# Window attention feeding a Mish FFN: attention matmuls in runs over two pairs of heads, two runs a chunk

## The chip, the cores and the metric

The kernel runs on one core of a Trainium2 chip. The metric is the device time of one execution in microseconds (us). The engines are called by their short names: PE (TensorE matmul; PEld is its weight load), DVE (VectorE), ACT (ScalarE), POOL (GpSimd) and SP (SyncE, which issues the DMAs).

## The reference

Sliding-window attention over q, k, v of 8 batches, 8 heads, 576 positions and 64 channels, and then a feed-forward network over the 4608 tokens of 512 channels:

```
mask = (rel >= 0) & (rel < 64)                 # a window of 64 positions
attn = softmax(where(mask, q @ k.T / 8, -1e9))  # sum + 1e-9 in the denominator
x    = (attn @ v) as [4608 tokens, 512 channels]
h    = x @ w_in                                 # 512 -> 2048
out  = (h * tanh(log1p(exp(h)))) @ w_out        # Mish, 2048 -> 512
```

All is in fp32. The kernel splits each FFN operand in a high and a low part (`xh`/`xl`, `wi_h`/`wi_l`, `gh`/`gl`, `wo_h`/`wo_l`) and sums three products of them.

## The kernel before, in words

The tokens are cut into 12 chunks of 384. A chunk has 16 FFN steps (f = 0 to 15). One step is 12 matmuls of `ffn_in` (L252) into one of two PSUM banks named `h_ps`, two Mish evaluations on ACT (L265, L266), a subtraction on POOL (L267), and, two steps later (`LAG`), 9 matmuls of `ffn_out` (L270) into the three accumulators `acc0`, `acc1`, `acc2`. So in step n of a chunk the matmuls that close the chunk before (its f = 15) run in step 1, and those with f = 0 of the new chunk open the accumulators again in step 2. In between `ffn_store` (L278) copies the accumulators to tiles `o`: ACT takes `acc0` and `acc2` (L283), DVE takes `acc1` (L285), and SP writes them out (L286).

The attention of chunk c is worked out while the FFN of chunk c-1 runs. From chunk 4 on it goes in "runs" (L178 to L213): the heads come in pairs, a chunk has 4 pairs with 3 squares of 128x128 scores each, and a run takes 4 squares of each of the two heads of a pair. `run_scores` puts 16 matmuls into two full banks of the pool `ps_at` (3 banks in all). `probs` (L143) takes each square: DVE adds the mask and finds the maximum (L161), ACT takes the exponential (L164), and then DVE normalises all at once (L151 to L153). `run_transpose` (L190) does a 32x32-block transpose on DVE (L193) into a tile `tr`, and `moves` (L186, L187) has SP issue 12 small DMAs from `tr` into `pT`. `run_values` (L196) then does 16 matmuls with `pT` into one bank `o_ps`, which ACT casts to `xh` (L212) and DVE subtracts to `xl` (L213).

The places of all these in the FFN's steps are fixed by `plan_runs` (L369): three runs a chunk, and the values of one run stand right ahead of the scores of the next, after `ffn_in` of a step and ahead of its `ffn_out`. The first run for a chunk stands three steps ahead of the chunk boundary (`ahead = 6` half steps), so the step order after it is: step 13, run, 14, 15, then 0, 1, 2 of the next chunk.

The tiles `pr` (L184), `tr` (L192), `o` (L280) and the staging of weights (L290) share one ring of three buffers in SBUF, tag `st`: a new tile takes the buffer that was handed out three tiles earlier, and its first writer waits for that tile's last reader. The readers of a `tr` are its 12 DMAs. In a run's order the ring hands out `pr`, `tr`; at a chunk boundary `o`, `o`, `o` for `acc0`, `acc1`, `acc2`. So the `o` for `acc2` gets the buffer of the `tr` of the run three steps ahead of the boundary.

Of the kernel before, what the change touches and what calls it, by code (L numbers as in the profile page):

```python
# [10 lines left out]
F32 = mybir.dt.float32  # L11
# [16 lines left out]
def tile_window_attn_mish_ffn(  # L28
# [44 lines left out]
    firsts = []  # L73
# [12 lines left out]
    SQ = DO // P
    pT_all = const.tile([P, 2 * HM * P], F32, name="pT")
    nc.gpsimd.memset(pT_all, 0.0)

    def pT_of(i, squares):  # L90
        n = squares * P
        return pT_all[:, i * n:(i + 1) * n].rearrange("p (r j i) -> p r j i", r=P // 32, i=32)

    pTs = itertools.cycle(pT_of(i, HM) for i in range(2))


    order = []
# [2 lines left out]
    def pe(*args, **kw):  # L100
        order.append(nc.tensor.matmul(*args, **kw).ins)  # L101
# [41 lines left out]
    def probs(c, s_ps, ms, pr, halves=False):  # L143

        ns = len(ms)
        mx = ap_.tile([P, 2 * SQ], F32, name="mx", bufs=3)
        sm = ap_.tile([P, 2 * SQ], F32, name="sm", bufs=3)

        def normal(js):
# [3 lines left out]
            nc.vector.tensor_tensor(pr[:, js, :], pr[:, js, :], sm[:, js].unsqueeze(2).to_broadcast([P, w, P]), ALU.mult)  # L153

        for h in range(2):
            for i, m in enumerate(ms):
                first = [(c * NB + 2 * m + par) % blocks_per_seq == 0 for par in range(2)]
                mk = firsts[first.index(True)] if any(first) else mask
                j = h * ns + i

                nc.vector.tensor_tensor_reduce(  # L161
                    out=pr[:, j, :], in0=s_ps[h][:, i, :], in1=mk,
                    op0=ALU.add, op1=ALU.min, scale=-0.125, scalar=3.0e38, accum_out=mx[:, j:j + 1])
                nc.scalar.activation(pr[:, j, :], pr[:, j, :], AF.Exp, bias=mx[:, j:j + 1], scale=-1.0,  # L164
                                     accum_out=sm[:, j:j + 1])
            if halves:
                normal(slice(h * ns, (h + 1) * ns))
        if not halves:
            normal(slice(0, 2 * ns))
        return pr  # L170

    def att_scores(c, p, tiles):
        s_ps = [bank(c, p, "s_ps").rearrange("p (m k) -> p m k", k=P) for _ in range(2)]
        for m in range(NM):
            products(tiles, m, [s[:, m, :] for s in s_ps])
        return probs(c, s_ps, range(NM), ap_.tile([P, HM, P], F32, name="pr", bufs=2), c == 0)

    def run_scores(c, i, qk):  # L178

        s_ps = [ps_at.tile([P, DO], F32, name="s_ps", tag="at").rearrange("p (m k) -> p m k", k=P) for _ in range(2)]  # L180
        ms = range(i * SQ, (i + 1) * SQ)
        for j, m in enumerate(ms):
            products(qk[m // NM], m % NM, [s[:, j, :] for s in s_ps])
        return probs(c, s_ps, [m % NM for m in ms], mp.tile([P, 2 * SQ, P], F32, name="pr", tag="st", bufs=3))  # L184

    def moves(pT, tr):  # L186
        return [nc.sync.dma_start(pT[k:k + 32, r // 32, :, :], tr[r:r + 32, k // 32, :, :])  # L187
                for r in range(0, P, 32) for k in range(0, P, 32) if 0 <= k - r % BLK <= BLK]

    def run_transpose(pr):  # L190
        pT = pT_of(0, 2 * SQ)
        tr = mp.tile([P, P // 32, 2 * SQ, 32], F32, name="tr", tag="st", bufs=3)  # L192
        nc.vector.transpose(tr.rearrange("p k j i -> p j k i"), pr.rearrange("p j (k i) -> p j k i", i=32))  # L193
        return pT, moves(pT, tr)

    def run_values(i, vs, pT, x):  # L196
        pT, moved = pT
        o_ps = ps_at.tile([P, DO], F32, name="o_ps", tag="at")
        for j in range(SQ):
            m = i * SQ + j  # L200
            for par in range(2):
                n = 2 * (m % NM) + par
                for h in range(2):
                    rows = slice(h * BLK, (h + 1) * BLK)
                    pe(o_ps[rows, (2 * j + par) * BLK:(2 * j + par + 1) * BLK], vs[m // NM][:, n, rows],
                       pT[:, 2 * par:2 * par + 2, h * SQ + j, :], start=True, stop=True)
                    for d in moved:
                        tc.add_manual_dep(order[-1], d.ins.name, SYNC, reason="values in one piece")
                    moved = []
        xh, xl = (t.rearrange("p c n -> p (c n)")[:, i * DO:(i + 1) * DO] for t in x)  # L210
        with tc.high_priority(offset=SOON):
            nc.scalar.copy(xh, o_ps)  # L212
            nc.vector.tensor_tensor(xl, o_ps, xh.bitcast(F32), ALU.subtract)  # L213

    def att_transpose(c, p, pr):
        pT = next(pTs)
# [15 lines left out]
        return pT, []  # L232

    def att_values(c, p, v_t, pT, x):
        pT, moved = pT
        xh, xl = x
        o_ps = bank(c, p, "o_ps")
        for n in range(NB):
            m, par = n // 2, n % 2
            for h in range(2):  # L240
                rows = slice(h * BLK, (h + 1) * BLK)
                pe(o_ps[rows, n * BLK:(n + 1) * BLK], v_t[:, n, rows],
                   pT[:, 2 * par:2 * par + 2, h * NM + m, :], start=True, stop=True)

                for d in moved:
                    tc.add_manual_dep(order[-1], d.ins.name, SYNC, reason="values in one piece")
                moved = []
# [66 lines left out]
    class Att:  # L314
# [30 lines left out]
                att_values(self.c, p, self.v[p], self.pT.pop(p), self.x)  # L345
            self.load(p + 2, "v")

        def run_scores(self, i):
            with in_order():
                self.pr[i] = run_scores(self.c, i, self.qk)  # L350
            self.load(i + 2, "qk")
            if i == RUNS - 1:
                self.load(NPAIR + 1, "qk")

        def run_transpose(self, i):
            if self.c == 4 and i == 0:
                nc.gpsimd.memset(pT_of(0, 2 * SQ), 0.0)
            self.pT[i] = run_transpose(self.pr.pop(i))

        def run_values(self, i):  # L360
            if self.x is None:
                self.x = tuple(xp.tile([P, NC_, CH], F32R, name=f"x{n}{self.c % 2}") for n in "hl")
            with in_order():
                run_values(i, self.v, self.pT.pop(i), self.x)
            self.load(i + 2, "v")
            if i == RUNS - 1:
                self.load(NPAIR + 1, "v")
# [141 lines left out]
```

## Time and profile before

| what | value |
|---|---|
| median of 3 timed runs | 952.58 us (951.73 to 952.84) |
| the profiled execution's own time | 954.34 us |
| its span, first to last instruction | 952.6 us |
| mean granted TensorE clock | 0.980 |
| HBM traffic over the span | 69 GB/s |

How to read the profile's lines: a group line gives the source line, engine, operation, output and input tiles and shapes, then count, total busy time, mean of one. A timeline line gives the start in us from the span's start, the duration, and what it is; `x12` means twelve like instructions that follow each other. The chain of waits is the chain of work that ended last, followed back from the end. A matmul in fp32 counts as two passes, so a run's 16 matmuls appear as `x32`.

### The profile page before, as it was taken

What the parts mean: (1) busy time and instruction counts of PE and PEld (TensorE: products, weight loads), DVE (VectorE), ACT (ScalarE), POOL (GpSimd) and SP (SyncE); (2) the same over time, 40 slices, a digit from 0 to 9 for tenths busy, and PEclk for the clock granted to TensorE, in tenths of its full rate; (3) what the DMA queues carried; (4) which work ended last, traced back from release to release, by engine and by line L of the source; (5) the groups of instructions that cost most, each with busy time, mean ns of one, the idle gap of its engine ahead of it and who ended that gap; (6) DMA issues with size and microseconds to landing.
All of it is one profiled execution on the core that took longest, in us unless ns stands there. A gap on an engine that the chain in (4) does not pass through costs nothing.

```text
span 952.6 us, 16654 instructions
## 1 busy us (share of the span) xinstructions
PE 917.1 (96%) x6408; PEld 816.4 (86%) x6408; DVE 301.0 (32%) x960; ACT 430.6 (45%) x1140; POOL 242.0 (25%) x241
## 2 busy tenths in 40 slices
PE   3779999999999999999999999999999999999998
PEld 2668999878889888899988998899988889988996
DVE  6899886142332122122122122222222222220000
ACT  4475333565654444344344345444444444442211
POOL 2234565202121222222222222222222222222221
PEclk9579999999999999999999999999999999999999
DMA  7454341131322222122023123122222222210000
GB/s 249 154 178 165 132 133 45 52 120 64 93 87 85 70 69 85 43 87 94 20 83 101 37 71 101 52 70 85 69 71 68 86 68 70 83 31 7 34 1 34
DMA packets 78031, 77.25 MB, mean 81 GB/s; under 512 B 8832, under 2 KB 69248, under 8 KB 77952
## 3 DMA queue, kind: packets, MB, share of 16 engines
q1 hardware_dynamic: 77952, 76.19, 25.6%
q8 instruction: 51, 0.84, 0.4%
q14 instruction: 28, 0.23, 0.1%
HBM read 56.10 MB, written 9.44 MB: 69 GB/s over the span
## 4 chain that ended last, share of the span: by engine, by line
PE 92%; DVE 4%; ACT 1%; DMA 1%; SPq 1%; issue 0%; ACTq 0%
PE h_ps L101 42%; PE acc L101 42%; PE o_ps L101 4%; PE s_ps L101 3%; DMA st<-w_in 1%; DVE pr L153 1%; DVE wa L301 1%; DVE pr L161 1%; ACT pr L164 1%; DVE wa L302 1%; SPq L187 0%; PE t_ps L228 0%; DVE wi_l L304 0%; ACT L164 0%; ACT L265 0%
## 5 line engine op out<-in xcount | busy, mean ns | idle before, releaser
L267 POOL TENSOR_TENSOR gl<-t,gh 128x384 fp32r<-128x384 f32 x192 | 199.0, 1037 | 614.4 <-ACT gh L266 606.0
L265 ACT ACTIVATE t<-h_ps 128x384 f32<-128x384 f32 x192 | 94.4, 491 | 396.7 <-PE h_ps L101 395.2
L101 PE MATMUL h_ps<-xh,wi_h 128*128 128x384 f32 x768 | 261.2, 340 | 0.0
L101 PE MATMUL h_ps<-xh,wi_l 128*128 128x384 f32 x768 | 260.3, 339 | 0.0
L101 PE MATMUL h_ps<-xl,wi_h 128*128 128x384 f32 x768 | 259.2, 337 | 0.0
L101 PE MATMUL acc<-wo_h,gh 128*128 128x512 f32 x576 | 230.3, 400 | 0.0
L101 PE MATMUL acc<-wo_l,gh 128*128 128x512 f32 x576 | 227.2, 394 | 0.0
L101 PE MATMUL acc<-wo_h,gl 128*128 128x512 f32 x576 | 224.6, 391 | 0.0
L101 PEld LDWEIGHTS h_ps<-xh,wi_h 128*128 128x128 f32 x768 | 145.3, 189 | 9.1 <-issue 0.7
L101 PEld LDWEIGHTS h_ps<-xl,wi_h 128*128 128x128 f32 x768 | 145.3, 189 | 7.2
L101 PEld LDWEIGHTS h_ps<-xh,wi_l 128*128 128x128 f32 x768 | 145.1, 189 | 0.0
L101 PEld LDWEIGHTS acc<-wo_h,gl 128*128 128x128 f32 x576 | 108.4, 188 | 24.6
L101 PEld LDWEIGHTS acc<-wo_h,gh 128*128 128x128 f32 x576 | 108.2, 188 | 22.3 <-issue 5.0
L101 PEld LDWEIGHTS acc<-wo_l,gh 128*128 128x128 f32 x576 | 108.6, 189 | 14.9
L164 ACT ACTIVATE pr<-pr,mx 128x128 f32<-128x128 f32 x288 | 111.7, 389 | 16.0 <-DVE mx L161 15.6
L213 DVE TENSOR_TENSOR xl<-o_ps,xh 128x512 fp32r<-128x512 f32 x24 | 16.6, 692 | 307.2 <-ACT xh L212 307.2
L266 ACT ACTIVATE gh<-h_ps 128x384 fp32r<-128x384 f32 x192 | 93.2, 485 | 0.0
L161 DVE CUSTOM_DVE_ANT_0 pr<-s_ps,mask 128x128 f32<-128x128 f32 x288 | 64.2, 286 | 32.2 <-PE s_ps L101 32.2
L285 DVE COPY o<-acc 128x512 f32<-128x512 f32 x12 | 8.3, 692 | 195.8 <-PE acc L101 195.8
L101 PE MATMUL s_ps<-k_t,q_t 64*64 64x128 f32 x1152 | 48.1, 292 | 13.5 <-DMA k_t<-kT 11.1
L101 PEld LDWEIGHTS o_ps<-pT,v_t 128*64 128x64 f32 x1152 | 40.8, 147 | 17.2 <-issue 8.6
L101 PEld LDWEIGHTS s_ps<-k_t,q_t 64*64 64x64 f32 x1152 | 36.6, 141 | 20.3 <-issue 8.4
(42 smaller groups left out, 572.1 us busy)
## 6 DMA issues: line engine op xcount, KB each, us to landing
v_t<-vN SPq DMA_DIRECT2D x48, 384.0 KB, 3.7
k_t<-kT SPq DMA_DIRECT2D x47, 224.0 KB, 4.1
out<-o SPq DMA_DIRECT2D x36, 256.0 KB, 2.1
pT<-tr SPq DMA_DIRECT2D x288, 32.0 KB, 1.8
q_t<-qT SPq DMA_DIRECT2D x47, 192.0 KB, 3.7
st<-w_in SPq DMA_DIRECT2D x16, 512.0 KB, 4.2
st<-w_out SPq DMA_DIRECT2D x16, 512.0 KB, 3.4
pT<-tr SPq DMA_DIRECT2D x48, 24.0 KB, 1.8
```

Source lines behind the costliest of these rows:

```text
L101: order.append(nc.tensor.matmul(*args, **kw).ins)
L153: nc.vector.tensor_tensor(pr[:, js, :], pr[:, js, :], sm[:, js].unsqueeze(2).to_broadcast([P, w, P]), ALU.mult)
L161: nc.vector.tensor_tensor_reduce(out=pr[:, j, :], in0=s_ps[h][:, i, :], in1=mk, op0=ALU.add, op1=ALU.min, scale=-0.125, scalar=3.0e38, acc ...
L164: nc.scalar.activation(pr[:, j, :], pr[:, j, :], AF.Exp, bias=mx[:, j:j + 1], scale=-1.0, accum_out=sm[:, j:j + 1])
L213: nc.vector.tensor_tensor(xl, o_ps, xh.bitcast(F32), ALU.subtract)
L265: nc.scalar.activation(t, h_ps, AF.Mish)
L266: nc.scalar.activation(gh, h_ps, AF.Mish)
L267: nc.gpsimd.tensor_tensor(gl, t, gh.bitcast(F32), ALU.subtract)
L285: nc.vector.tensor_copy(o, acc[t])
L301: nc.vector.scalar_tensor_tensor(a, hi, 0xC0000000, a, ALU.bitwise_and, ALU.bitwise_or)
L302: nc.vector.scalar_tensor_tensor(a, lo, 29, a, ALU.logical_shift_right, ALU.bitwise_or)
```

## The change

From chunk 4 on a run covers two whole pairs of heads (6 squares a head), and there are two runs a chunk in place of three.

- The scores need three banks. `run_scores` takes two full banks of `ps_at`, and for the remaining two squares of each head one more bank of `ps_at` for one head and one of the two `h_ps` banks for the other. It is 24 matmuls.
- The values are 24 matmuls. The first four blocks of 64 columns go to a bank of `ps_at`, the other eight to an `h_ps` bank. DVE copies and subtracts the first part; ACT casts and DVE subtracts the second, as before.
- `probs` is called for the second pair of the run first, with the squares in the `h_ps` bank leading, and then for the first pair. Each call normalises its own 6 squares.
- The tile `pr` leaves the ring `st` for a pool of its own (2 buffers); `tr` stays in the ring. A run has two transposes, two `tr` tiles and 24 DMAs of 24 KB where it had 12 of 32 KB.
- `pT` is two fixed tiles instead of one tile cut in two ways; its second clearing goes.
- `plan_runs` spaces the two runs evenly. The first still stands three steps ahead of the chunk boundary; the second moves to five steps behind it. Before, the second and third stood two and eight steps behind it.

The core of the diff:

```diff
-    def run_scores(c, i, qk):
-        s_ps = [ps_at.tile([P, DO], F32, name="s_ps", tag="at").rearrange("p (m k) -> p m k", k=P) for _ in range(2)]
-        ms = range(i * SQ, (i + 1) * SQ)
...
-        return probs(c, s_ps, [m % NM for m in ms], mp.tile([P, 2 * SQ, P], F32, name="pr", tag="st", bufs=3))
+    def run_scores(c, qk):
+        full, half = [], []
+        names = ["s_ps"] * 2
+        full = [squares(ps_at.tile([P, DO], F32, name=n, tag="at")) for n in names]
+        half = [squares(pool.tile([P, DO], F32, name=n, tag=tag)) for n, pool, tag in
+                zip(names, (ps_at, ps_h), ("at", "h_ps"))]
...
+        late = [(h, m) for h in (1, 0) for m in (1, 2)] + [(0, 0), (1, 0)]
+        second = probs(c, s_ps[1], [late])
+        return [probs(c, s_ps[0], [sum(HEADS, [])]), second]
...
-        tr = mp.tile([P, P // 32, 2 * SQ, 32], F32, name="tr", tag="st", bufs=3)
+        pT = next(pTs)
+        tr = mp.tile([P, P // 32, HM, 32], F32, name="tr", tag="st", bufs=3)
...
+        o_ps = [ps_at.tile([P, DO], F32, name="o_ps", tag="at")[:, :cut], ps_h.tile([P, DO], F32, name="o_ps", tag="h_ps")]
...
+        value_products(vs[0], pTs_[0], blocks[:NB])
         with tc.high_priority(offset=SOON):
-            nc.scalar.copy(xh, o_ps)
-            nc.vector.tensor_tensor(xl, o_ps, xh.bitcast(F32), ALU.subtract)
+            nc.vector.tensor_copy(xh[:, :cut], o_ps[0])
+            nc.vector.tensor_tensor(xl[:, :cut], o_ps[0], xh[:, :cut].bitcast(F32), ALU.subtract)
+        value_products(vs[1], pTs_[1], blocks[NB:])
+        with tc.high_priority(offset=SOON):
+            nc.scalar.copy(xh[:, cut:], o_ps[1])
+            nc.vector.tensor_tensor(xl[:, cut:], o_ps[1], xh[:, cut:].bitcast(F32), ALU.subtract)
...
+        def run_transpose(self, p):
+            for q in (p, p + 1):
+                self.pT[q] = run_transpose(self.pr.pop(q))
...
-            at = [begin + 2 * round((end - begin) * i / RUNS / 2) for i in range(RUNS + 1)]
-            for i in range(RUNS):
+            step = (end - begin) / (NPAIR // 2)
+            for p in range(0, NPAIR, 2):
+                at = begin + p // 2 * step
+                events.extend([(at, 2, self.run_scores, p), (at + 0.4 * step, 1, self.run_transpose, p),
+                               (at + step, 0, self.run_values, p)])
```

Two places in the order of instructions are shown, since the prediction rests on them. The first is SP's queue around a chunk boundary of the kernel before: a run's 12 moves into `pT` stand ahead of the three writes of `o`.

```order
L187 DMA pT<-tr 32x256 x12
L131 DMA v_t<-vN 128x6x128 x2
L122 DMA q_t<-qT 128x384
L124 DMA k_t<-kT 128x448
L187 DMA pT<-tr 32x256 x12
L286 DMA out<-o 128x512 x3
L131 DMA v_t<-vN 128x6x128
```

The same place in the changed kernel, where the two `pT` tiles have numbers:

```order
L190 DMA pT_106<-tr 32x192 x12
L190 DMA pT_107<-tr 32x192 x12
L126 DMA v_t<-vN 128x6x128 x2
L117 DMA q_t<-qT 128x384
L119 DMA k_t<-kT 128x448
L117 DMA q_t<-qT 128x384
L119 DMA k_t<-kT 128x448
L190 DMA pT_106<-tr 32x192 x12
L190 DMA pT_107<-tr 32x192 x12
L287 DMA out<-o 128x512 x3
```

Between the transposes of the run ahead of a boundary and the writes of `o` there are now 24 moves on SP where there were 12. The second place is ACT's queue at the same boundary, with the counters that each instruction waits for (`DMAHW0` to `7` count landings of SP's DMAs, the others count an engine's instructions; the number behind a tile's name tells allocations apart). Before, with `t` and `gh` the two Mish evaluations of a step:

```order
L265 ACTIVATE t<-h_ps 128x384 [waits PE_49]
L266 ACTIVATE gh<-h_ps 128x384 [waits Pool_49]
L283 COPY o<-acc_3051 128x512 [waits DMAHW4_49,DMAHW3_49,DMAHW5_49,DMAHW2_49,DMAHW6_49,DMAHW1_49,DMAHW7_49,DMAHW0_49,PE_49]
L283 COPY o<-acc_3053 128x512 [waits DMAHW3_49,DMAHW4_49,DMAHW2_49,DMAHW5_49,DMAHW1_49,DMAHW6_49,DMAHW0_49,DMAHW7_49,DVE_49,PE_49]
L265 ACTIVATE t<-h_ps 128x384 [waits PE_49]
L266 ACTIVATE gh<-h_ps 128x384 [waits Pool_49]
```

In the changed kernel:

```order
L266 ACTIVATE t<-h_ps 128x384 [waits PE_49]
L267 ACTIVATE gh<-h_ps 128x384 [waits Pool_49]
L284 COPY o<-acc_3027 128x512 [waits DMAHW4_49,DMAHW3_49,DMAHW5_49,DMAHW2_49,DMAHW6_49,DMAHW1_49,DMAHW7_49,DMAHW0_49,PE_49]
L266 ACTIVATE t<-h_ps 128x384 [waits PE_49]
L267 ACTIVATE gh<-h_ps 128x384 [waits Pool_49]
L284 COPY o<-acc_3029 128x512 [waits DMAHW4_49,DMAHW3_49,DMAHW5_49,DMAHW2_49,DMAHW6_49,DMAHW1_49,DMAHW7_49,DMAHW0_49,DVE_49]
L266 ACTIVATE t<-h_ps 128x384 [waits PE_49]
```

The copy of `acc2` (here `acc_3053` and `acc_3029`) waited for DMAs in both. In both, the ring `st` gives its `o` the buffer of the last `tr` of the run ahead of the boundary, so the landings that it waits for are those of that `tr`: the 12th move before, the 24th now. The two Mish evaluations of step 2 moved ahead of this copy.

More of the change, by code (lines that the diff above doesn't have):

```diff
@@ L83, in tile_window_attn_mish_ffn @@
     wo_l = const.tile([P, NF, DO], F32R, name="wo_l")
[L86 to L94, printed above, removed]
+    pTs = [const.tile([P, P // 32, HM, 32], F32, name=f"pT{i}") for i in range(2)]
+    for t in pTs:
+        nc.gpsimd.memset(t, 0.0)
+    pTs = itertools.cycle(pTs)
     order = []
@@ L141, in products, with probs @@
                q_t[rows, n * BLK:(n + 1) * BLK], k_t[rows, n * BLK:n * BLK + P], start=True, stop=True)
[L143 to L149, printed above, removed]
+    def probs(c, s_ps, turns):
+        pr = ap_.tile([P, HM, P], F32, name="pr", bufs=2)
+        mx = ap_.tile([P, HM], F32, name="mx", bufs=3)
+        sm = ap_.tile([P, HM], F32, name="sm", bufs=3)
+        for turn in turns:
+            js = [h * NM + m for h, m in turn]
+            for j, (h, m) in zip(js, turn):
+                first = [(c * NB + 2 * m + par) % blocks_per_seq == 0 for par in range(2)]
+                mk = firsts[first.index(True)] if any(first) else mask
+                nc.vector.tensor_tensor_reduce(
+                    out=pr[:, j, :], in0=s_ps[h][m], in1=mk,
+                    op0=ALU.add, op1=ALU.min, scale=-0.125, scalar=3.0e38, accum_out=mx[:, j:j + 1])
+                nc.scalar.activation(pr[:, j, :], pr[:, j, :], AF.Exp, bias=mx[:, j:j + 1], scale=-1.0,
+                                     accum_out=sm[:, j:j + 1])
+            js = slice(min(js), max(js) + 1)
             w = js.stop - js.start
@@ L153, in normal @@
             nc.vector.tensor_tensor(pr[:, js, :], pr[:, js, :], sm[:, js].unsqueeze(2).to_broadcast([P, w, P]), ALU.mult)
[L155 to L167, printed above, removed]
@@ L168, in probs, with squares @@
-        if not halves:
-            normal(slice(0, 2 * ns))
-        return pr
+        return pr
+    HEADS = [[(h, m) for m in range(NM)] for h in range(2)]
+    def squares(bank_):
+        return bank_.rearrange("p (m k) -> p m k", k=P)
     def att_scores(c, p, tiles):
-        s_ps = [bank(c, p, "s_ps").rearrange("p (m k) -> p m k", k=P) for _ in range(2)]
+        s_ps = [squares(bank(c, p, "s_ps")) for _ in range(2)]
+        s_ps = [[s[:, m, :] for m in range(NM)] for s in s_ps]
         for m in range(NM):
-            products(tiles, m, [s[:, m, :] for s in s_ps])
@@ L176, in att_scores @@
-        return probs(c, s_ps, range(NM), ap_.tile([P, HM, P], F32, name="pr", bufs=2), c == 0)
-    def run_scores(c, i, qk):
-        s_ps = [ps_at.tile([P, DO], F32, name="s_ps", tag="at").rearrange("p (m k) -> p m k", k=P) for _ in range(2)]
-        ms = range(i * SQ, (i + 1) * SQ)
-        for j, m in enumerate(ms):
-            products(qk[m // NM], m % NM, [s[:, j, :] for s in s_ps])
-        return probs(c, s_ps, [m % NM for m in ms], mp.tile([P, 2 * SQ, P], F32, name="pr", tag="st", bufs=3))
+            products(tiles, m, [s[m] for s in s_ps])
@@ new lines, in att_scores @@
+        return probs(c, s_ps, HEADS if c == 0 else [sum(HEADS, [])])
+    def run_scores(c, qk):
[4 more added lines that the diff above has]
+                zip(names, (ps_at, ps_h), ("at", "h_ps"))]
+        s_ps = [[[full[h][:, m, :] for m in range(NM)] for h in range(2)],
+                [[full[h][:, NM, :]] + [half[h][:, m, :] for m in range(NM - 1)] for h in range(2)]]
+        for tiles, s in zip(qk, s_ps):
+            for m in range(NM):
+                products(tiles, m, [s[h][m] for h in range(2)])
+        late = [(h, m) for h in (1, 0) for m in (1, 2)] + [(0, 0), (1, 0)]
+        second = probs(c, s_ps[1], [late])
+        return [probs(c, s_ps[0], [sum(HEADS, [])]), second]
@@ L190, in run_transpose, with value_products @@
     def run_transpose(pr):
-        pT = pT_of(0, 2 * SQ)
-        tr = mp.tile([P, P // 32, 2 * SQ, 32], F32, name="tr", tag="st", bufs=3)
+        pT = next(pTs)
+        tr = mp.tile([P, P // 32, HM, 32], F32, name="tr", tag="st", bufs=3)
         nc.vector.transpose(tr.rearrange("p k j i -> p j k i"), pr.rearrange("p j (k i) -> p j k i", i=32))
         return pT, moves(pT, tr)
-    def run_values(i, vs, pT, x):
+    def value_products(v_t, pT, blocks):
         pT, moved = pT
[L198 to L210, printed above, removed]
-        with tc.high_priority(offset=SOON):
-            nc.scalar.copy(xh, o_ps)
-            nc.vector.tensor_tensor(xl, o_ps, xh.bitcast(F32), ALU.subtract)
@@ new lines, in value_products, with run_values @@
+        for n, to in enumerate(blocks):
+            m, par = n // 2, n % 2
+            for h in range(2):
+                rows = slice(h * BLK, (h + 1) * BLK)
+                pe(to[rows, :], v_t[:, n, rows], pT[:, 2 * par:2 * par + 2, h * NM + m, :], start=True, stop=True)
+                for d in moved:
+                    tc.add_manual_dep(order[-1], d.ins.name, SYNC, reason="values in one piece")
+                moved = []
+    def run_values(p, vs, pTs_, x):
+        cut = 2 * CH - DO
+        o_ps = [ps_at.tile([P, DO], F32, name="o_ps", tag="at")[:, :cut], ps_h.tile([P, DO], F32, name="o_ps", tag="h_ps")]
+        blocks = [o[:, n:n + BLK] for o in o_ps for n in range(0, o.shape[1], BLK)]
+        xh, xl = (t.rearrange("p c n -> p (c n)")[:, p * CH:(p + 2) * CH] for t in x)
+        value_products(vs[0], pTs_[0], blocks[:NB])
+        with tc.high_priority(offset=SOON):
+            nc.vector.tensor_copy(xh[:, :cut], o_ps[0])
[4 more added lines that the diff above has]
+            nc.vector.tensor_tensor(xl[:, cut:], o_ps[1], xh[:, cut:].bitcast(F32), ALU.subtract)
@@ L234, in att_values @@
     def att_values(c, p, v_t, pT, x):
-        pT, moved = pT
         xh, xl = x
         o_ps = bank(c, p, "o_ps")
[L238 to L247, printed above, removed]
+        value_products(v_t, pT, [o_ps[:, n:n + BLK] for n in range(0, CH, BLK)])
         with tc.high_priority(offset=SOON):
@@ L346, in values, with run_scores, run_values @@
             self.load(p + 2, "v")
-        def run_scores(self, i):
+        def run_scores(self, p):
+            ps = (p, p + 1)
             with in_order():
[L350 to L360, printed above, removed]
+                self.pr.update(zip(ps, run_scores(self.c, [self.qk[q] for q in ps])))
+            for q in ps:
+                self.load(q + 2, "qk")
+        def run_transpose(self, p):
+            for q in (p, p + 1):
+                self.pT[q] = run_transpose(self.pr.pop(q))
+        def run_values(self, p):
             if self.x is None:
                 self.x = tuple(xp.tile([P, NC_, CH], F32R, name=f"x{n}{self.c % 2}") for n in "hl")
+            ps = (p, p + 1)
             with in_order():
[L364 to L367, printed above, removed]
+                run_values(p, [self.v[q] for q in ps], [self.pT.pop(q) for q in ps], self.x)
+            for q in ps:
+                self.load(q + 2, "v")
         def plan_runs(self, begin, end):
-            at = [begin + 2 * round((end - begin) * i / RUNS / 2) for i in range(RUNS + 1)]
-            for i in range(RUNS):
-                events.extend([(at[i], 2, self.run_scores, i), (at[i] + 0.6 * (at[i + 1] - at[i]), 1, self.run_transpose, i),
-                               (at[i + 1], 0, self.run_values, i)])
+            step = (end - begin) / (NPAIR // 2)
[3 more added lines that the diff above has]
+                               (at + step, 0, self.run_values, p)])
         def plan(self, begin, step, turn=0.6, lag=1):
@@ L382, in tile_window_attn_mish_ffn @@
     events = []
-    RUNS = NPAIR * NM // SQ
     def run(slot):
```

## The prediction

> **What bounds the kernel now.** I read the page first: its span, its busy shares, and the chain that ended last.
>
> ```profile
> span 952.6 us, 16654 instructions
> PE 917.1 (96%) x6408; PEld 816.4 (86%) x6408; DVE 301.0 (32%) x960; ACT 430.6 (45%) x1140; POOL 242.0 (25%) x241
> PE 92%; DVE 4%; ACT 1%; DMA 1%; SPq 1%; issue 0%; ACTq 0%
> ```
>
> PE is the chain. The stretch from 100 us to the end, where the change lies, has PE busy for 844.56 of 852.6 us at the full clock (PE's busy time is the second number, the granted clock stands after POOL's):
>
> ```profile
> 100.00:952.60 852.60, 844.56 (x5809) 756.24 (x5808) 218.77 (x726) 375.39 (x985) 209.14 (x200) 1.00 0.22 69
> ```
>
> So only two things count: how long PE takes over a chunk, and whether anything makes it wait. The second view is the chain in order of time through the run that stands ahead of a chunk boundary, up to the next run:
>
> ```profile
> 349.98 1.08 PE o_ps L101 x32
> 351.06 1.03 PE s_ps L101 x32
> 352.10 2.28 PE acc L101 x9
> 354.38 2.08 PE h_ps L101 x12
> 356.47 2.06 PE acc L101 x9
> 358.53 2.11 PE h_ps L101 x12
> ...
> 368.97 2.06 PE acc L101 x9
> 371.03 2.11 PE h_ps L101 x12
> 373.13 1.08 PE o_ps L101 x32
> ```
>
> and three runs later, from the same view of a later stretch:
>
> ```profile
> 423.61 1.08 PE o_ps L101 x32
> ```
>
> A chunk takes 423.61 - 349.98 = 73.63 us on PE, with no gap. An FFN step without a run is 2.06 + 2.11 = 4.17 us, sixteen are 66.72, so three runs cost 6.91 us, or 2.30 each. How much of that is streaming and how much is changing over from large to small matmuls? The timeline of a run and the durations of a single pass tell:
>
> ```profile
> 400.38 1.15 PE L101 MATMUL o_ps<-pT,v_t 128*64 128x64 f32 x32
> 401.47 1.10 PE L101 MATMUL s_ps<-k_t,q_t 64*64 64x128 f32 x32
> L101 PE MATMUL o_ps<-pT,v_t x128: 222/222/270, 400.4 to 474.9; 128*64 128x64 f32 x128
> L101 PE MATMUL s_ps<-k_t,q_t x128: 269/269/320, 401.5 to 475.9; 64*64 64x128 f32 x128
> ```
>
> From the first start to the last, 31 steps of a value pass take 1.15 - 0.22 = 0.93 us (0.030 each), and 31 of a score pass 1.10 - 0.27 = 0.83 (0.027 each). So 16 more passes of each kind add 16 x (0.030 + 0.027) = 0.91 us.
>
> **The change part by part: PE's own work.** The passes stay, there are only fewer runs. A run of 48 + 48 passes costs 2.30 + 0.91 = 3.21 us, two cost 6.42, and three of the old ones 6.91: 0.49 us less a chunk. Eight chunks (4 to 11) save 3.9 us. At the first run of chunk 4 the order puts two `ffn_out` matmuls among the scores, a changeover more: what a run costs beyond its streaming is 2.30 - 32 x 0.057 = 0.48 us, so I add 0.4 once. The second half of a run's values has a wait of its own for 12 landings, in the middle of PE's queue. The landings are long past (below), so it costs only its decoding. No row shows that in the middle of a run. The nearest is the waits view of four runs, where PEld stands idle 0.25 us ahead of each run's first load, which has such a wait:
>
> ```profile
> PEld o_ps L101 <- issue: 1.0, 4, 0.3
> ```
>
> From above that is 0.25 us in each of 16 runs, 4.0 us; from below nothing, and no gain either, since a wait speeds nothing. I take nothing: the idle time at a run's start also holds the changeover, and here there is none.
>
> PE's new waits for banks have room. The half bank in `ps_at` needs DVE's two operations on 256 columns of the first values: 16 passes (0.48 us), a hand-off of 0.1 and two thirds of the 0.955 us that 768 columns take in a row below, so about 1.2 us into the run. Its first score comes after 48 value and 32 score passes, at 2.3. The bank in `h_ps` needs the Mish ahead of the run, which ends before the cast at 351.11, 1.1 us into it. DVE's and ACT's small changes lie beside PE and are costed at nothing; the cover is that DVE is busy 32% and ACT 45%. ACT's block of exponentials grows from 8 to 12, and the Mish behind it must end before the third `ffn_in` after the run:
>
> ```profile
> 351.11 0.59 ACT L212 CAST xh<-o_ps 128x512 fp32r<-128x512 f32 x1 [0.22 <-PE o_ps L101]
> 353.01 0.40 ACT L164 ACTIVATE pr<-pr,mx 128x128 f32<-128x128 f32 x1
> 355.72 0.39 ACT L164 ACTIVATE pr<-pr,mx 128x128 f32<-128x128 f32 x1
> 357.51 0.49 ACT L265 ACTIVATE t<-h_ps 128x384 f32<-128x384 f32 x1
> ```
>
> The first and last of the 8 exponentials are 2.71 us apart, 0.387 each. The cast comes 16 value passes later (0.48 us), four more exponentials take 1.55, so that Mish starts at 359.54 and ends by 360.5; PE needs it at 362.69 + 0.91 = 363.6 (one `h_ps` group after 358.53, shifted by the longer run). 3 us to spare.
>
> **What is late next: the moves on SP.** The run at 349.98 stands three steps ahead of a boundary. These rows follow it, on DVE, SP and ACT:
>
> ```profile
> 356.68 1.22 DVE L153 TENSOR_TENSOR pr<-pr,sm 128x1024 f32<-128x1024 f32 x1
> 357.94 1.25 DVE L193 STREAM_TRANSPOSE tr<-pr 128x1024 f32<-128x1024 f32 x1
> 359.21 7.49 SPq L187 DMA_DIRECT2D pT<-tr  x12
> 369.76 0.59 ACT L283 COPY o<-acc 128x512 f32<-128x512 f32 x1
> 371.06 0.59 ACT L283 COPY o<-acc 128x512 f32<-128x512 f32 x1 [0.71 <-DVE o L285]
> ```
>
> Twelve moves take SP 7.49 us, 0.62 each. Is it their size? In chunk 3 the moves already have 24 KB, and the issue takes the same; the landing too (median from issue to landing, last column):
>
> ```profile
> 243.47 7.48 SPq L187 DMA_DIRECT2D pT<-tr  x12
> pT<-tr SPq DMA_DIRECT2D x288, 32.0 KB, 1.8
> pT<-tr SPq DMA_DIRECT2D x48, 24.0 KB, 1.8
> ```
>
> So SP is paid by the move, and 24 of them take twice as long. Before, the last landed at about 366.1 + 1.8 = 367.9, and the copy of `acc2` that waits for it came at 371.06: 3 us to spare. Now, on the same clock: the last exponential starts at 355.72 + 0.48 + 1.55 = 357.75, DVE's normalising follows it by 356.68 - 355.72 = 0.96, and its two operations have these lengths for 768 columns:
>
> ```profile
> L153 DVE TENSOR_TENSOR pr<-pr,sm 128x768 f32<-128x768 f32 x12 | 11.5, 955 | 0.3
> L221 DVE STREAM_TRANSPOSE tr<-pr 128x768 f32<-128x768 f32 x4 | 3.9, 978 | 0.1
> ```
>
> The first transpose ends at 357.75 + 0.96 + 0.96 + 0.04 + 0.98 = 360.7. SP issues from there on; the 24th move starts at 360.7 + 23 x 0.624 = 375.05 and lands at 376.85. Only then may ACT copy `acc2`: until 377.45. PE wants that bank for f = 0 of the new chunk: the flush of the old one ends at 371.03 + 0.91 = 371.94, an `h_ps` group (2.11) and six of the nine `ffn_out` matmuls (1.37) later it is 375.4. It waits 2.05 us by these rows, and three hand-offs (move to ACT, ACT to PE, and the twelve-wide waits' decoding) at about 0.1 each make it 2.4. I take 2.4, with 1.9 and 2.9 as ends. Before, a run stood at 373.13 and gave this copy 2 us more of cover; the new plan has none there. SP's other work behind the moves has time: the writes of `o` are waited for by no one soon, and the next loads need the next run on PE, half a chunk (37 us) after this one. The copy of `acc1` waits for the 12th move (360.7 + 6.9 + 1.8 = 369.4) and is not late. There are eight such boundaries, chunks 3 to 10: 8 x 2.4 = 19.2 us.
>
> **And PE's clock.** A stop of PE can cost more than its length. Stretches of 3.4 us from the head of the kernel, in the same columns:
>
> ```profile
> 60.40:63.80 3.40, 2.23 (x24) 1.68 (x25) 3.40 (x13) 2.73 (x5) 2.64 (x3) 1.00 0.76 257
> 63.80:67.20 3.40, 3.40 (x37) 2.57 (x37) 3.40 (x13) 3.39 (x13) 0.50 (x1) 1.00 0.42 125
> 70.70:74.10 3.40, 2.20 (x27) 1.69 (x26) 2.97 (x11) 3.36 (x6) 1.80 (x3) 0.99 0.64 257
> 74.10:77.50 3.40, 3.40 (x16) 2.26 (x16) 3.40 (x15) 2.19 (x12) 0.00 (x0) 0.50 0.44 130
> 77.50:80.90 3.40, 3.40 (x41) 3.20 (x37) 3.10 (x6) 1.92 (x4) 1.63 (x1) 1.00 0.42 123
> 200.40:203.80 3.40, 2.26 (x31) 1.46 (x29) 2.37 (x11) 1.64 (x9) 0.00 (x0) 1.00 0.53 158
> 203.80:207.20 3.40, 3.29 (x39) 3.02 (x39) 2.02 (x12) 3.38 (x14) 0.00 (x0) 1.00 0.31 104
> ```
>
> With 1.20 us idle the next stretch ran at 0.50; with 1.17 and 1.14 it ran on at 1.00. One fully busy stretch brought the clock back. A stop of 2.4 us is twice that, so nearly wherever it falls one stretch has 1.2 us idle, and the next gives half its work: 3.4 x 0.5 = 1.7 us. Eight times: 13.6 us. That price rests on one stretch, so its ends are 0 and 13.6.
>
> The Trainium skill, "TensorE: Matmul & The Clock Gate", Part 1, has the clock fall back only after at least one whole idle window of about 3.4 us. The trace here disagrees, with a fall after 1.20 us of idling at 74.10. By the Trainium skill the sum would lack the 13.6 us; that is a rival below.
>
> **The sum.** -3.9 + 0.4 + 19.2 + 13.6 = +29.3 us on the span of 952.6 us, which gives 981.9; the median of the timed runs, 952.58, is the same, and the profiled execution's own 954.34 is 1.8 above it, so I forecast the median from the span: 982.
>
> **The rivals.**
> The stop without the clock: PE waits 2.4 us at each boundary and runs on at full speed. For it: two stretches with 1.17 and 1.14 us idle that cost nothing, and a boundary between 1.17 and 1.20 that hangs on one case. Against: 2.4 is far above either. It gives 952.6 + 15.7 = 968.3. The rule of the Trainium skill, above, would have this one.
>
> The stop is not there, and the kernel is faster. What decides is SP's pace: the copy is in time if the 24th move lands by 374.5, so at (374.5 - 1.8 - 360.7) / 23 = 0.52 us a move or less. For it: nothing but that ACT could find these waits fulfilled by another order at the boundary. Against: 0.62 in both sizes. It gives 952.6 - 3.5 = 949.1.
>
> The stop is longer: landing and hand-offs at their upper end and idling in two stretches, 8 x (2.9 + 2.5) - 3.5 = +39.7, or 992.3. That the change does less than it says is no rival: the order shows the runs on PE as described.
>
> **How the numbers follow.** Forecast (stop and clock) 0.62; its own range, with 1.9 to 2.9 us of stop and 1.5 to 2.0 of clock, is 8 x 3.4 - 3.5 to 8 x 4.9 - 3.5, so 976 to 988. Stop without clock 0.16; longer stop 0.06; no stop 0.14; between these, within 0.2% (about 1.9 us, what a measurement of this kernel can tell from no change) 0.02. The range from 966 to 989 takes in the first two and leaves out about 0.2. Faster 0.14, same 0.02, slower 0.84.
>
> **What would show it.** Right: in ACT's waits the copy of `acc2` waits for `pT<-tr` eight times, about 2 us each behind the step's Mish; PE idles 2 to 2.5 us ahead of an `acc` matmul once a chunk; a stretch of 0.50 follows in the clock; a run costs 3.2 us on PE. Wrong: no idle PE between 300 and 860 us, or 24 moves in much less than 15 us on SP. If PE idles but the clock stays, only the 13.6 us fall; if PE idles inside the runs, the bank waits or the second wait in the values were underrated.

## The result, and the profile after

The changed kernel takes 976.58 us (median; 975.89 to 977.26) where the kernel before takes 952.15 (951.55 to 952.84). The ratio is 1.0256, 95% interval 1.0239 to 1.0274: slower by 24.4 us. The forecast was 982, its range 966 to 989. Of the executions in the experiments below one, the profiled execution of E7, took 2291.6 us where its four others took 1006 to 1009, so its profile is not read and E10 profiles that kernel again. The head of the changed kernel's page, and its chain by engine:

```profile
span 973.6 us, 16757 instructions
PE 921.2 (95%) x6408; PEld 820.3 (84%) x6408; DVE 311.3 (32%) x1016; ACT 404.5 (42%) x1116; POOL 242.2 (25%) x241
PE 69%; SPq 12%; ACT 7%; DVE 7%; DMA 2%; issue 2%; ACTq 0%
```

PE's busy time hardly changed (917.1 before), but its share of the chain fell from 92% to 69%. The chain in order of time shows what took the rest: from the run three steps ahead of a boundary, over the transposes and the first and last of SP's moves in the chain, to the new chunk (start, length, what):

```profile
346.36 1.57 PE o_ps L96 x48
...
356.07 0.99 DVE tr L196
...
357.07 0.51 SPq L190
...
370.93 0.44 SPq L190
371.37 2.04 issue
...
373.57 0.59 ACT o L284
...
374.21 0.97 PE acc L96 x3
375.18 3.26 PE h_ps L96 x12
378.44 2.40 PE acc L96 x9
```

SP issues a move every 0.63 us from 357.07 on, so the 24th starts at 357.07 + 23 x 0.63 = 371.56, and with the page's median of 1.8 us from issue to landing it is there at 373.4. The 2.04 us at 371.37 are ACT's wait for it. Then ACT copies `acc2`, and only then may PE open it. At 375.18 a group of twelve takes 3.26 us in place of 2.11, and the nine behind it 2.40 in place of 2.06: the clock. The waits of the whole execution say how much PE stood (in total, times, longest):

```profile
PE acc L96 <- ACT o L284: 20.2, 8, 3.8
ACT o L284 <- DMA pT<-tr: 18.3, 7, 3.6
```

Eight stops, 20.2 us. The timeline has each of them, in brackets behind PE's first pass on `acc2`. Here are the first three; the others took 3.09, 2.25, 2.31, 2.42 and 3.79.

```profile
298.32 0.50 PE L96 MATMUL acc<-wo_h,gh 128*128 128x512 f32 x1 [0.74 <-ACT o L284]
374.21 0.50 PE L96 MATMUL acc<-wo_h,gh 128*128 128x512 f32 x1 [2.38 <-ACT o L284]
452.47 0.50 PE L96 MATMUL acc<-wo_h,gh 128*128 128x512 f32 x1 [3.25 <-ACT o L284]
```

Why 2.3 at some boundaries and 3.1 to 3.8 at three? SP's moves in the timeline, ahead of the second and the third stop:

```profile
357.07 15.07 SPq L190 DMA_DIRECT2D pT<-tr  x24
434.42 16.05 SPq L190 DMA_DIRECT2D pT<-tr  x24
```

24 moves take 15.07 us, 0.628 each, or about one more (16.05 here, 15.88 ahead of the fourth stop, 16.32 ahead of the eighth). The DMA view of 434 to 451 us shows what came between:

```profile
q8 instruction: 1, 0.02, 0.5%
```

A 16 KB packet of instructions was loaded in that window, and in those of the two other long rows; in the five others no packet of this queue was. Within the row at 434.42 one issue of SP lasted 1.57 us in place of 0.59.

The spans of two executions are not compared here, since what stands ahead of chunk 2 takes anything from 207.1 to 211.9 us in eleven profiles, whichever the kernel. Lengths of chunks are steadier, from the first pass of `ffn_in` to that of the next chunk (the third kernel is the first experiment):

| chunk | before | changed | changed, no stops (E1) |
|---|---|---|---|
| 2 | 77.05 | 78.47 | 78.17 |
| 3 | 73.63 | 74.28 | 73.12 |
| 4 | 73.63 | 77.38 | 73.12 |
| 5 | 73.63 | 76.70 | 73.12 |
| 6 | 73.63 | 78.12 | 73.12 |
| 7 | 73.63 | 77.29 | 73.12 |
| 8 | 73.63 | 75.77 | 73.12 |
| 9 | 73.63 | 75.87 | 73.12 |
| 10 | 72.61 | 77.19 | 71.66 |
| sum | 665.07 | 691.07 | 661.67 |

The changed kernel loses 26.0 us here. Without stops it would win 3.4, so stops and clock cost 29.4. Of these, 20.2 are standing. Starting again costs some 0.33 more at each stop: chunks 5, 8 and 9, with no clock loss, are 3.58, 2.65 and 2.75 longer than E1's, for stops of 3.25, 2.31 and 2.42, and the three passes at 374.21 take 0.97 where 0.69 is usual. In chunk 3 it is 0.42 (1.16 longer for 0.74), so 2.7 in all. Chunk 2, without such a stop, differs by 0.3. The rest, 6.1, falls to the four stretches at half speed: 1.5 each, as in the rows above ((3.26 - 2.11) + (2.40 - 2.06) = 1.49).

Which stops drew them? Stretches of the clock in the changed kernel (PE's busy time second, granted clock behind POOL's):

```profile
372.20:375.60 3.40, 1.39 (x7) 1.26 (x8) 0.00 (x0) 0.59 (x1) 0.24 (x1) 0.95 0.65 233
375.60:379.00 3.40, 3.40 (x12) 3.29 (x11) 0.00 (x0) 0.53 (x2) 0.00 (x0) 0.50 0.06 19
447.30:450.70 3.40, 1.91 (x10) 1.32 (x8) 0.00 (x0) 0.87 (x2) 1.00 (x1) 0.95 0.16 43
450.70:454.10 3.40, 1.63 (x8) 1.50 (x9) 0.00 (x0) 0.59 (x1) 0.00 (x0) 0.95 0.63 239
454.10:457.50 3.40, 3.40 (x19) 3.03 (x18) 0.00 (x0) 0.87 (x2) 0.99 (x1) 0.95 0.00 0
```

After 2.01 us idle (3.40 - 1.39) the next stretch ran at 0.50. The longer stop at 452 fell across two stretches, idle 1.49 and 1.77, and cost the clock nothing. So 1.2 us, the limit that the forecast took, is too low here. (The full clock reads 0.95 in this execution and 1.00 in others; a step takes 2.11 + 2.06 us in both.)

### The profile page after: what moved, and what is told of

Same layout as the page of the kernel before. It is cut to its first block, busy times and chain, and to the rows that moved or that the text cites. A ratio compares the mean times of both kernels' runs of the same rounds, so it can differ in the third digit from the quotient of the medians.

```text
span 973.6 us, 16757 instructions
## 1 busy us (share of the span) xinstructions
PE 921.2 (95%) x6408; PEld 820.3 (84%) x6408; DVE 311.3 (32%) x1016; ACT 404.5 (42%) x1116; POOL 242.2 (25%) x241
## 4 chain that ended last, share of the span: by engine, by line
PE 69%; SPq 12%; ACT 7%; DVE 7%; DMA 2%; issue 2%; ACTq 0%
PE h_ps L96 32%; PE acc L96 31%; SPq L190 12%; ACT pr L151 5%; PE o_ps L96 4%; PE s_ps L96 2%; DVE pr L157 2%; DMA pT<-tr 1%; ACT L151 1%; DVE tr L196 1%; DVE pr L148 1%; DVE wa L303 1%; DVE wa L302 1%; DMA st<-w_in 1%; PE t_ps L239 1%
## 5 line engine op out<-in xcount | busy, mean ns | idle before, releaser
L96 PE MATMUL acc<-wo_h,gh 128*128 128x512 f32 x576 | 231.5, 402 | 20.2 <-ACT o L284 20.2
L96 PEld LDWEIGHTS acc<-wo_h,gh 128*128 128x128 f32 x576 | 108.8, 189 | 44.4 <-ACT o L284 23.6
L219 DVE CAST xh<-o_ps 128x256 fp32r<-128x256 f32 x16 | 6.8, 425 | 356.0 <-PE o_ps L96 356.0
L151 ACT ACTIVATION_READ_ACCUMULATOR pr<-pr,mx 128x1 f32 x288 | 54.0, 187 | 0.0
```

## The experiments

Three questions: is the stop the ring's wait for the 24th move, and nothing else at the boundary or in the runs; is it SP's issues that make that move late; and what does the clock count?

**E1: `o` for `acc2` waits for the first `tr`.**

```diff
-        for t in range(NTT):
-            o = mp.tile([P, DO], F32, name="o", bufs=3, tag="st")
+        both = mp.tile([P, 2, DO], F32, name="o", bufs=3, tag="st")
+        last = mp.tile([P, DO], F32, name="o", bufs=3, tag="st")
+        for t in range(NTT):
+            o = both[:, t, :] if t < 2 else last
```

> The changed kernel, but the first two of the three output copies of a chunk share one 4 KB buffer of the ring st, so that the third copy (acc2) takes over the buffer of the run's first tr (12th move) and not that of its second (24th move). Theory (acc2's copy waits for the 24th move): the 12th move lands about 2 us before the copy, so the eight stops of PE (20.2 us in all in the changed kernel's profile) and the clock's four half-speed stretches (4 x 1.7) go: 976.6 - 20.2 - 6.8 = 949.6. Rival 1 (the time is lost in the longer runs: bank waits, second wait inside the values): the stops stay or move into the runs, 970 or more. Rival 2 (a new wait takes over, now on the 12th move or on the shared buffer): between 955 and 970, with ACT's copies idle behind another move.

Measured: 948.43 us, ratio to the kernel before 0.9957 (0.9943 to 0.9972). The chain across the same boundary is PE alone, and ACT copies `acc0` and `acc2` as soon as they are closed:

```profile
367.38 2.06 PE acc L96 x9
369.44 2.11 PE h_ps L96 x12
```

```profile
368.18 0.59 ACT L286 COPY o<-acc 128x512 f32<-128x512 f32 x1
369.48 0.59 ACT L286 COPY o<-acc 128x512 f32<-128x512 f32 x1 [0.71 <-DVE o L288]
```

No stop is left, though SP still issues its 24 moves, until 374.3 us here (one of them 1.62 us long):

```profile
358.19 16.13 SPq L190 DMA_DIRECT2D pT<-tr  x24
```

Runs, banks, second wait and boundary are as in the changed kernel. So the loss is the reuse of one buffer, and rival 1 is out.

**E2: the run one step earlier.**

```diff
-    ahead = 6
+    ahead = 8
```

> The changed kernel with ahead = 8 for 6: every chunk's first run stands four steps ahead of the boundary and not three, one step (4.17 us) earlier, nothing else. Theory: the 24th move lands 4.17 us earlier against PE's need of acc2, so a stop of 2.3 to 3.8 us is gone at all eight boundaries: 976.6 - 20.2 - 6.8 = 949.6, and the same to within 1 us as the kernel with the shared output buffer. Rival 1 (loss inside the runs): 976 still. Rival 3 (the stop belongs to the boundary itself, three copies in a row on ACT and DVE, whatever the moves do): 976 still.

Measured: 955.77 us, ratio 1.0032 (1.0019 to 1.0044). The eight boundaries lost their stops as expected (no gap above 0.3 us behind chunk 2), but the total missed by 6 us. PE's timeline has a stop at another place, in chunk 2:

```profile
276.03 1.25 PE L96 MATMUL o_ps<-pT,v_t 128*64 128x64 f32 x19 [4.46 <-DMA pT<-tr]
```

The earlier end pressed chunk 3's attention, which goes by another plan, into less room; its last values waited for their own moves (one issue of 1.97 us among them), and a stretch at half speed followed. Chunk 2 took 85.03 us in place of E1's 78.17.

**E3: another number of moves at each boundary.**

```diff
+    DOSE = {5: -1, 6: -2, 7: -3, 8: -4, 9: 2, 10: 4, 11: 6}
...
+               for r, k in todo[:len(todo) + min(dose, 0)]]
+        for i in range(max(dose, 0)):
+            nc.sync.dma_start(ident[32 * (i % 4):32 * (i % 4) + 32, i // 4 * BLK:(i // 4 + 1) * BLK], tr[0:32, i % 4, 0:2, :])
```

> The changed kernel with another number of moves behind the second tr of each chunk's first run, boundary by boundary: 12 (chunk 4's run), 11, 10, 9, 8, 14, 16, 18 (chunk 11's run). Where moves are left out the values read old blocks, and the extra ones go to a buffer nobody reads. Theory (SP pays 0.63 us by the move, and PE waits for the last): the stops of PE are about 0.7, 1.7, 1.0, 0.4, 0.0, 3.6, 4.8, 6.1 us, each 0.9 to 1.3 longer where a 16 KB instruction packet falls among the moves; a stop changes by 0.63 us a move. Rival (the bytes or the landing count, not the issue): the extra moves carry a third of the bytes, so the stops grow by 0.2 us a move or not at all. Clock: by my forecast's rule (half speed after 1.2 us of idling in one 3.4 us stretch) a drop follows every stop of 2.4 us or more; by a limit near 2 us, which the changed kernel's profile suggests (drops after 2.01, 2.04, 3.09, 3.40; none after 1.79, 1.65, 1.46), the stops of 3.6, 4.8 and 6.1 drop and those up to 1.7 don't; by a limit of a whole idle stretch only the longest drops, if any.

Measured: 978.08 us, one execution. PE's stops in its timeline (ahead of these stands one of 0.79, and the fifth, with 8 moves behind the second `tr`, is not there):

```profile
375.66 0.50 PE L97 MATMUL acc<-wo_h,gh 128*128 128x512 f32 x1 [1.68 <-ACT o L289]
450.91 0.50 PE L97 MATMUL acc<-wo_h,gh 128*128 128x512 f32 x1 [1.88 <-ACT o L289]
525.82 0.50 PE L97 MATMUL acc<-wo_h,gh 128*128 128x512 f32 x1 [1.50 <-ACT o L289]
676.23 0.79 PE L97 MATMUL acc<-wo_h,gh 128*128 128x512 f32 x1 [3.55 <-ACT o L289]
756.82 0.79 PE L97 MATMUL acc<-wo_h,gh 128*128 128x512 f32 x1 [4.81 <-ACT o L289]
839.09 0.80 PE L97 MATMUL acc<-wo_h,gh 128*128 128x512 f32 x1 [7.42 <-ACT o L289]
```

Expected were 0.7, 1.7, 1.0, 0.4, (0.0,) 3.6, 4.8, 6.1. Five agree to within 0.1. The others are 0.9, 1.1 and 1.3 longer, and SP's rows say why:

```profile
434.30 14.55 SPq L192 DMA_DIRECT2D pT<-tr  x22
584.48 12.54 SPq L192 DMA_DIRECT2D pT<-tr  x20
816.93 16.40 SPq L192 DMA_DIRECT2D pT<-tr  x24
```

20 moves take 12.54, 0.627 each. By that 22 and 24 would take 13.8 and 15.0, and they took 0.8 and 1.4 more; the 21 took 14.18, 1.0 more. An instruction packet fell into these three windows and not into that of the 20. The extra moves carry a third of the bytes, and two of them more still lengthen the stop by 4.81 - 3.55 = 1.26 us, so it is the issue that counts. The clock fell after the stops of 3.55, 4.81 and 7.42 and after none of the smaller ones.

**E4: the shared buffer in the kernel before.** The same edit as in E1.

> The kernel before with the same shared buffer for the first two output copies: the control for the shared buffer itself. Theory: the kernel before has no stop at its boundaries (3 us to spare), so there is nothing to win: 952, within 1 us of it. Rival (the shared buffer helps by itself, for example through fewer waits of SP or earlier loads): 949 or less.

Measured: 951.20 us, ratio 0.999 (0.998 to 0.9999). Its chunks have the length of the kernel before, 73.63, so what it seems to gain is not in the chunks. The shared buffer is no gain by itself.

**E5: the earlier run without touching chunk 3's plan.**

```diff
         else:
+            ahead = 8
             atts[c].plan_runs(begin, starts[c] - ahead)
```

> The changed kernel with its runs one step earlier (ahead = 8) only from the run on that stands ahead of the second boundary; the plan of chunk 3 and the run ahead of its boundary stay as they are. It asks where the 7 us come from that the kernel with ahead = 8 throughout lost to the one with the shared output buffer (955.8 against 948.4). Theory: all of it is chunk 3's attention, whose plan was pressed together by the earlier end (one stop of 4.46 us at 276 and the half-speed stretch behind it); with that plan as it was, the seven later stops are gone, the first (0.74) stays: 948.4 + 0.7 = 949.1. Rival: the earlier runs cost something at every boundary that no idle PE shows: 954 or more.

Measured: 949.85 us, ratio 0.9976 (0.9964 to 0.9988). The first stop stayed, 0.79 us, the seven others are gone, and chunk 2 takes 78.53. So E2's 6 us were chunk 3's.

**E6: half of the moves from another queue.**

```diff
-                self.pT[q] = run_transpose(self.pr.pop(q))
+                self.pT[q] = run_transpose(self.pr.pop(q), nc.gpsimd if q == p + 1 else nc.sync)
```

> The changed kernel with the 12 moves of each run's second tr issued by GpSimd and not by SP, the ring as in the changed kernel. Theory (the stop is SP's 24 issues in a row): the two dozens go out side by side, the last lands some 7 us earlier if GpSimd needs about as long for an issue as SP, and the stops are gone: 948 to 950. Rival 1 (GpSimd issues more slowly or its issues hold back the subtraction that PE needs for every ffn_out): new stops of PE inside the steps behind the run, 955 to 1000. Rival 2 (the landing, not the issue, is what is slow): the stops stay, 976.

Measured: 948.30 us, ratio 0.996 (0.9945 to 0.9974). No stop at a boundary. The rows of POOL and of SP behind one run, and the issues' medians to landing:

```profile
357.56 5.88 POOL L190 DMA_DIRECT2D pT<-tr  x12 [0.32 <-DVE tr L196]
```

```profile
356.43 7.50 SPq L190 DMA_DIRECT2D pT<-tr  x12
```

```profile
pT<-tr SPq DMA_DIRECT2D x240, 24.0 KB, 1.8
pT<-tr POOLq DMA_DIRECT2D x192, 24.0 KB, 1.7
```

The two dozens go out side by side, and both land as fast as before: the landing was never late, the queue was. POOL's subtraction is held up for those 5.88 us, which PE felt once (chunk 8 took 73.73). The ring and its wait are as in the changed kernel, so the wait costs nothing once the issues end earlier. The Trainium skill, "DMA: Bandwidth & Descriptors", Rules for kernel authors, has it that spreading DMAs over the engines' queues gains no bandwidth and only saves the sequencer's issue time; the trace agrees, with landings of 1.8 and 1.7 us as before, and here the issue time was all.

**E7 and E10: four moves more at every boundary.** `DOSE` of E3 set to 4 for every chunk. E10 is the same kernel again.

> The changed kernel with four more moves (a third of the bytes each, to a buffer nobody reads) behind the second tr of each chunk's first run: SP issues 28 moves where it issued 24. Theory: each of the eight stops grows by 4 x 0.63 = 2.5 us, to 3.3 to 6.3 us, 40.4 in all. Clock: by a limit of about 1.8 us of idling in a 3.4 us stretch, and by my forecast's 1.2 too, half speed follows every one of them, 8 x 1.7 = 13.6: 948.4 + 40.4 + 13.6 = 1002. If a whole idle stretch were needed, only the stops that happen to cover one would lose it, about 3 of 8: 994.

> The kernel with 28 moves once more, for its profile: it took 1007 us where 1002 were worked out from eight stops of 40.4 us in all and eight stretches at half speed. Expected: the stops as worked out (3.3 to 6.3 us), and more than eight half-speed stretches, about eleven, since a stop of 4.8 us can leave two stretches short of work; if the stops are longer instead, an issue costs more than 0.63 us when 28 follow each other.

Measured: E7 1007.25 us, ratio 1.0576 (1.0552 to 1.0601); E10 1005.67, one execution. The waits of E10:

```profile
PE acc L97 <- ACT o L289: 40.7, 8, 6.0
```

The stops are 40.7 us as worked out (40.4). Half speed follows all eight, and in four of them for two stretches, twelve in all where eight had been counted. The chunks 3 to 10 are 56.7 us longer than E1's: 40.7, 2.6 for starting again, and 13.4 for the clock, 1.1 a stretch (in the second of two, PE stands for a part of it). A whole stretch idle isn't needed.

**E9: two moves fewer at every boundary.** `DOSE` set to -2.

> The changed kernel without the last two of the 12 moves of the second tr of each chunk's first run (the values read old blocks there): SP issues 22 moves where it issued 24. It asks for the clock's price by itself. Theory: each stop is 1.27 us shorter than in the changed kernel's profile, so 0.0 to 2.5 us, 10.6 in all. By a limit near 1.8 us of idling in one 3.4 us stretch of 128-row passes, none or one of them is followed by half speed: 948.4 + 10.6 + 0 to 1.7 = 959 to 961. By my forecast's limit of 1.2 us, four or five of them are: 966 to 968.

Measured: 965.76 us, ratio 1.0154 (1.0137 to 1.0171). The total lies where the forecast's limit of 1.2 us would put it, but the trace says otherwise: PE's stops are 10.8 us, about as worked out, and half speed followed two of them, not four or five.

```profile
PE acc L97 <- ACT o L289: 10.8, 7, 2.4
```

What the expectation lacked is the 0.3 for starting again at each boundary (2.4) and a second half-speed stretch (1.5). The chunks 3 to 10 are 16.0 us longer than E1's, and 10.8 + 2.4 + 2 x 1.5 makes 16.2. One of the two falls:

```profile
447.20:450.60 3.40, 1.31 (x6) 0.77 (x5) 0.00 (x0) 1.10 (x3) 1.00 (x1) 1.00 0.47 172
450.60:454.00 3.40, 3.40 (x12) 3.20 (x11) 0.00 (x0) 0.00 (x0) 0.00 (x0) 0.51 0.21 81
```

2.09 us idle, and the clock falls. The other came after 2.13; after the stretch from 525.7 us, with 1.24 idle, it stayed up.

**E8: a busy PE with few rows.** In E1's kernel, step 8 of chunks 5, 7 and 9:

```diff
+            rows, cols = {5: (32, P), 7: (P, 32), 9: (P, P)}[c]
+            spare = ps_h.tile([P, CH], F32, name="spare", tag="h_ps")
+            for _ in range(80):
+                pe(spare[:cols, :], wi_h[:rows, f, 0, :cols], xh[:rows, 0, :], start=True, stop=True)
```

> The kernel with the shared output buffer (no stops), with 80 additional matmuls in a row, 384 columns streamed each, whose product nobody reads, in one step of three chunks: with 32 rows of the weights in chunk 5, with 32 columns of them in chunk 7, with all 128 x 128 in chunk 9. It asks what counts as idle for the clock. Over the windows of six profiles so far, half speed follows where the busy time weighted by the rows in use (rows / 128) is under 0.47 of a stretch, while the plain idle time does not separate them (1.20 us idle fell beside 64-row passes, 1.79 us did not beside 128-row ones). By the rows: PE is never idle, yet the clock falls to half in the 32-row block (0.25 a stretch) after one stretch and stays there to its end, so that its 13.7 us take 20 or more; it stays at full speed in the other two. By rows times columns: it falls in both narrow blocks. By idle time alone, my forecast's rule: it falls in none.

Measured: 999.96 us, one execution. The first block, in PE's timeline, and the clock of stretches in it:

```profile
472.53 21.79 PE L96 MATMUL spare<-xh,wi_h 32*128 32x384 f32 x80
```

```profile
474.10:477.50 3.40, 3.40 (x22) 3.40 (x21) 0.00 (x0) 0.00 (x0) 0.48 (x1) 1.00 0.12 30
477.50:480.90 3.40, 3.40 (x12) 3.40 (x12) 0.00 (x0) 0.00 (x0) 0.00 (x0) 0.50 0.15 40
```

and the blocks with 32 columns and with the full array:

```profile
642.30:656.20 13.90, 13.90 (x82) 8.73 (x81) 0.00 (x0) 0.87 (x2) 1.01 (x1) 1.00 0.12 33
802.40:816.40 14.00, 14.00 (x82) 14.00 (x82) 0.00 (x0) 0.87 (x2) 1.01 (x1) 1.00 0.12 32
```

PE is busy throughout all three. With 32 rows the clock falls after one stretch and the block makes its chunk 23.6 us longer; with 32 columns and with all, 13.9. Neither idle time nor rows times columns can say that; the rows can.

## Why the prediction was right, and where it was not

**PE's own work** was right. In the changed kernel a run is 1.55 + 1.51 us and 0.21 of the group behind it:

```profile
309.74 1.55 PE o_ps L96 x48
311.29 1.51 PE s_ps L96 x48
312.80 2.27 PE acc L96 x9
```

3.27 where 3.21 was worked out; by the length of E1's chunks it is 3.20 ((73.12 - 66.72) / 2). With the stops away, E1's chunks are 0.51 us shorter than before (0.49 predicted). All in all the runs bring 3.4 us (665.07 - 661.67; 3.5 predicted). The second wait in the values and the two borrowed banks cost nothing that the chunk lengths show.

**The late move** was right in place, cause and size. E1 takes the buffer away, E5 the time, E6 the queue, and the stop goes each time; E3 moves it by 0.63 us a move. On the run's clock the first move was put 10.7 us behind the run's start (360.7 - 349.98) and came 10.71 behind (357.07 - 346.36). The four undisturbed stops are 2.25 to 2.42 us for 2.4. The rival without a stop asked for 0.52 us a move; it is 0.63. The three hand-offs, put at about 0.1 each without a row for it, are about 0.25 together: 373.4 to 373.57 from the landing to ACT's copy, and 374.16, its end, to 374.21.

**Three sizes inside the 19.2 us were off, and partly cancel.** The first of the eight is 0.74 and not 2.4, because the run ahead of it has 24 value passes and not 48 (PE, then SP):

```profile
271.93 0.92 PE L96 MATMUL o_ps<-pT,v_t 128*64 128x64 f32 x24 [0.98 <-DMA pT<-tr]
```

```profile
281.10 15.08 SPq L190 DMA_DIRECT2D pT<-tr  x24
```

Its moves begin 9.2 us behind its start, 1.5 earlier than the others. Three are 0.7 to 1.4 longer, since an instruction load fell among the moves. And each restart costs 0.33 (0.42 at the first) that is not in the idle time, a term that the forecast did not have. Together 20.23 + 2.73 = 22.96 for 19.2.

**The clock was the step that failed in size:** 13.6 us were forecast, eight times 1.7, and 6.1 came. The price of a stretch was nearly right (1.5), their number wrong: four stops of eight drew one. The forecast's limit, 1.2 us idle, came from the head of the kernel, where passes of 64 rows stand in the stretch. The rows of `s_ps` passes alone, in the kernel before, beside the same two stretches that the prediction shows:

```profile
70.70:74.10 3.40, 1.58 (x24) 1.09 (x22) 0.63 (x3) 0.99 0.64 257
200.40:203.80 3.40, 1.15 (x24) 0.91 (x24) 0.70 (x4) 1.00 0.53 158
```

They use half of the rows. If they count half, the first stretch has 2.20 - 1.58 / 2 = 1.41 us of work, 0.41 of it, and the second 2.26 - 1.15 / 2 = 1.69, 0.50. So the mark lies between 0.41 and 0.50 of a stretch. In the FFN all rows are in use, so there it is reached at 1.7 to 2.0 us of idling; above, 1.77 cost nothing and 2.01 did. The stops lie around that mark, and where a stretch begins decides: of a stop of 2.38 us, 2.01 lay in one stretch, and the clock fell; 3.25 us across two cost nothing. An estimate from these rows, with 1.8 us as the limit: a stop of 2.4 us that may begin anywhere leaves 1.8 us in one stretch of 3.4 at (3.4 - 2.4 + 2 x 0.6) / 3.4 = 0.65 of the places, so five of eight would have been the better count. The Trainium skill's rule, at least one whole idle window ("TensorE: Matmul & The Clock Gate", Part 1), is not borne out either: 2.01 us idle was enough here, and E8's fall came with none.

**The sum:** -3.5 + 19.2 + 13.6 = +29.3 was forecast. The chunks say -3.4 + 23.0 + 6.1 + 0.3 (chunk 2) = +26.0, the timed medians +24.4; what stands ahead of chunk 2 varies too much to tell the 1.6 us between them apart. On the chunks an error of 7.5 in the clock and one of 3.8 the other way in the stops left 3.3 us too much. So the mechanism was right, and that the number came within 5.4 us of 976.58 is in part luck: two errors of opposite sign. The rival of a stop without clock, 968.3, was too low, since it lacks the 6.1 of the clock and the stops' excess.

## What to carry to other kernels

When a change makes a producer slower in one piece, look at who inherits its buffers: a ring hands the wait to an engine that has nothing to do with the data. Three ways took the stop away here: another sharing of the ring (E1), an earlier start (E2, E5), a second queue (E6). Which of them is free is found by asking which leaves the other stages as they were: the earlier start did not, at first. With the stop away the change is a small gain: 948.43 (E1) and 948.30 (E6) against 952.5 for the kernel before, both faster by 0.4%.

## What the runs showed of the hardware

- Half speed of PE follows a 3.4 us stretch when the busy time, weighted by the rows in use (rows / 128), is under about 0.47 of it. Counted from the clock records and the passes of eleven profiles, the falls at a kernel's end left out: of 53 stretches followed by half speed, 52 lie at or below 0.473 and one at 0.480; the others, more than 2800, lie at or above 0.476. Only the 32-row block of E8 was made for this question; the mark itself is read off the other stretches. What brings the clock back is left open.
- SP needs 0.627 us to issue a move between 32 and 32 partitions, whether it carries 32, 24 or 8 KB; POOL needs 0.49 (5.88 / 12).
- A 16 KB instruction packet goes with an issue of SP that is 0.3 to 1.4 us longer. In the eleven profiles 109 issues of moves lasted more than 0.7 us, and each has the start of such a packet between 0.52 us ahead of its own start and 0.18 us behind it. It lengthened three of eight stops in the changed kernel. That the load is what holds the issue is argued from their falling together, not tried.
